# Second mixture of experts: row scatters spread over the next stage, weight sums in bfloat16 and one step later, the first expert's weight steps moved

## The chip, the cores and the metric

One core of one Trainium2 chip. The metric is the device time of one execution in microseconds (us). TensorE (PE) does the matrix products, VectorE (DVE), ScalarE (ACT) and GpSimd (POOL) the elementwise work; SyncE (SP) issues most transfers, POOL the indirect ones. Each engine takes its instructions in the order in which they are written and waits on semaphores.

## The reference, cut to what matters

The program does three things in a row: attention in chunks of 64, a mixture of experts in which each token goes to one expert, and a second mixture in which every token goes through every expert, with weights from 8 normalisations of rows and columns. The change touches only the second:

```
def _moe2_ref(x, w_gate, w1, w2):      # x: 2304 x 512, w1: 8 x 512 x 1024, w2: 8 x 1024 x 512
    logits = x @ w_gate
    P = np.exp(logits - logits.max())
    for _ in range(8):
        P /= P.sum(1, keepdims=True) + 1e-09
        P /= P.sum(0, keepdims=True) + 1e-09
        P *= N / E
    out = np.zeros((N, D))
    for e in range(E):
        out += P[:, e:e + 1] * (np.maximum(x @ w1[e], 0.0) @ w2[e])
```

The products are made from 16-bit halves: an operand is scaled by a power of two and split into a high and a low float16 part, and three of the four products of parts are added up. The power of two comes from the sum of the squares of the whole weight matrix.

## The kernel before, in words

**Loops.** The second mixture runs over 8 experts, `x = 0..7` in the code; an expert has 3 stages, `s = 0..2`, of 768 tokens. A stage has a first half (`x @ w1`, seven block products for each of four column groups `q`, 28 of six matmuls each, L1104) and a second half (times `w2`). The first expert (`plain`) does its second half as six plain products, `t = 0..5` (`second`, L1233, 24 matmuls of 512 columns each); the other seven do it by Strassen's scheme (`strassen`, L1189): seven products of 36 matmuls, in the order m = 1, 5, 6, 3, 7, 2, 4.

**Steps.** What else must be done is hung on numbered steps of a stage: `plan(s, i, f)` puts f behind step i of stage s, and `tick` runs it there. Steps 0 to 27 are the block products of the first half, step 28 + n follows the n-th product of the second half. Nothing runs by itself at a step: the number only sets where the instructions stand in the order of their engines.

**Elementwise work of the first half.** For a column group, ACT copies products out of PSUM to a tile `tq` (L1144 to L1146), DVE adds others to them (L1119), ACT makes the high parts `eh` (L1109), and the low parts `el` are made by DVE (`low`, L1112) or, from the second expert on, four of seven by POOL (`rest`, L1116). There are two `tq` tiles, taken in turn by the column groups; a group's copy waits until the last reader of the group two before it is done.

**The next expert's weights.** While expert x runs, matrices "b" (`w2`) and "a" (`w1`) of expert x + 1 are loaded to one staging buffer (L155, SP queue), squared and summed by ACT in four quarters (`w_stat`, L166, one column of `mx` each), summed over the partitions by a float32 matmul against ones (`w_scale`, `over_partitions`, L175: lhsT `ones32`, four columns, into the PSUM bank `p_l`), turned to a power of two by DVE (`w_scale2`, L189 and L89 to L92), and split in four pieces (`w_quad`): POOL makes the block sums into a `tq` tile (L252), ACT the high parts (L273), DVE the low parts (L274). Two of the four pieces of "b" are parked in DRAM (`b_away`, L1253) and fetched back at the next expert (`b_back`). For the first expert of this mixture the "b" matrix is split plainly during its first stage (`w_split`).

**The first expert** also turns the tokens by transposing transfers, makes the seven token blocks (`x_first` in its first stage by PE, step numbers in `build`; `x_sums` after), and computes the row and column normalisations (`sink_...`, DVE with an L175 sum on PE, the `scs` ones).

**The end.** Each stage's rows of the sum `acc` get the last expert's share by `into` (L1171). In the last expert `scatter` (L1176) follows at once: an indirect transfer from POOL for each of the stage's six row blocks, three behind product m = 2 and three behind m = 4.

## Time and profile before

| what | value |
|---|---|
| three runs | 1826.03, 1829.67, 1833.31 us (median 1829.67) |
| the profiled execution | 1826.54 us, span 1824.8 us |
| mean granted TensorE clock | 0.975 of full speed |
| busy in the span | PE 94%, PE weight loads 68%, DVE 66%, ACT 52%, POOL 39% |
| chain that ended last | PE 65%, DVE 4%, ACT 4% |

The span is the profiled execution from its first to its last instruction; the 1.7 us around it are the start and the end. Where PE is at work nearly all the time, what counts is where it stands still, and why. Times in the rows are from the span's start; the second mixture begins at about 414 us.

### The profile page before, as it was taken

Reading aid. Unit: us, or ns where it says so; the run is one execution under the profiler, and the core shown is the slowest. Engines: PE = TensorE matmul, PEld = TensorE weight load, DVE = VectorE, ACT = ScalarE, POOL = GpSimd, SP = SyncE. Lnnn points to the kernel's source line nnn. Section 1 sums busy time; section 2 is a strip of 40 time slices with the busy share of each in tenths; the row PEclk is TensorE's granted clock in tenths of the full one; section 3 lists DMA queues with packets and bytes.
Section 4 is the critical chain, followed back from the end, with each engine's and each line's share of the span. In section 5 each row is a group of like instructions: output and inputs, shape, how many; then the busy total and the mean of one; then the engine's idle time right before and its main releaser. Section 6 shows DMA issues by size and latency. Waiting matters only on the chain.

```text
span 1824.8 us, 33023 instructions
## 1 busy us (share of the span) xinstructions
PE 1715.4 (94%) x13025; PEld 1236.3 (68%) x13025; DVE 1199.6 (66%) x2341; ACT 957.5 (52%) x1806; POOL 709.9 (39%) x750
## 2 busy tenths in 40 slices
PE   7878999888899899999999999999999999999985
PEld 6766666655355477777777777777777777777654
DVE  5996657755456576676677667667766776675652
ACT  7964656754334465564465445555644655452330
POOL 1344335540011144353455345453433543443432
PEclk9978999999999899999999999999999999999997
DMA  9846566834324222332314224323313142222200
GB/s 237 209 158 219 164 191 162 226 118 131 127 44 155 83 91 80 121 124 92 128 62 168 87 82 161 108 82 108 138 71 128 62 170 99 92 97 79 79 35 35
DMA packets 140905, 219.17 MB, mean 120 GB/s; under 512 B 62881, under 2 KB 81393, under 8 KB 140721
## 3 DMA queue, kind: packets, MB, share of 16 engines
q1 hardware_dynamic: 133728, 198.92, 33.9%
q0 software_dynamic: 5360, 17.24, 2.9%
q8 instruction: 115, 1.88, 0.4%
q10 hardware_dynamic: 1632, 0.56, 0.1%
q14 instruction: 70, 0.57, 0.1%
HBM read 167.56 MB, written 41.91 MB: 115 GB/s over the span
## 4 chain that ended last, share of the span: by engine, by line
PE 65%; DVE 4%; ACT 4%; issue 2%; DMA 1%; POOL 0%; POOLq 0%; DVEq 0%; ACTq 0%
PE p_m L1104 34%; PE p_m L1189 26%; PE p_m L1233 4%; ACT wsq L166 3%; DVE tq L1122 2%; DVE acc L1171 1%; DMA out_dram<-acc,rk 1%; ACT eh L1109 1%; DVE wall L274 0%; PE p_m L992 0%; POOL el L1116 0%; PE p_l L175 0%; DVE tq L1119 0%; DVE el L1112 0%; ACT wall L231 0%
## 5 line engine op out<-in xcount | busy, mean ns | idle before, releaser
L1104 PE MATMUL p_m<-x,wall 128*128 128x384 f16 x4032 | 673.0, 328 | 18.2 <-ACT tq L1144 13.7
L1104 PEld LDWEIGHTS <-wall 128*128 128x128 f16 x4032 | 396.2, 98 | 279.7 <-issue 25.7
L1189 PE MATMUL p_m<-wall,eh 128*128 128x256 f16 x3528 | 580.6, 273 | 0.0
L1116 POOL TENSOR_TENSOR el<-tq,eh 128x384 f16<-128x384 f32 x336 | 344.6, 1053 | 558.8 <-ACT eh L1109 558.4
L1189 PE MATMUL p_m<-wall,el 128*128 128x256 f16 x1764 | 480.8, 273 | 0.0
L1109 ACT ACTIVATE eh<-tq 128x384 f16<-128x384 f32 x540 | 273.9, 522 | 200.9 <-DVE tq L1122 101.4
L1189 PEld LDWEIGHTS <-eh 128*128 128x128 f16 x3528 | 345.3, 98 | 44.3
L1171 DVE SCALAR_TENSOR_TENSOR acc<-p_m,cf,acc 128x256 f32<-128x256 f32 (+1 forms) x378 | 175.8, 521 | 181.1 <-PE p_m L1189 181.1
L1119 DVE TENSOR_TENSOR tq<-p_m,tq 128x384 f32<-128x384 f32 x288 | 159.1, 556 | 149.5 <-PE p_m L1104 143.6
L1189 PEld LDWEIGHTS <-el 128*128 128x128 f16 x1764 | 172.6, 98 | 19.9
L1112 DVE SCALAR_TENSOR_TENSOR el<-tq,eh 128x384 f16<-128x384 f32 x204 | 171.6, 844 | 8.3 <-ACT eh L1109 6.9
L1122 DVE SCALAR_TENSOR_TENSOR tq<-tq 128x384 f32<-128x384 f32 x252 | 133.0, 553 | 2.9
L1144 ACT COPY tq<-p_m 128x384 f32<-128x384 f32 x96 | 45.6, 475 | 153.6 <-PE p_m L1104 141.5
L742 PEld LDWEIGHTS <-wall 128*128 128x128 f16 x1152 | 106.0, 99 | 22.2 <-issue 7.0
L742 PE MATMUL p_p<-xT,wall 128*128 128x256 f16 x768 | 88.9, 277 | 6.3 <-DMA xT<-xg 2.1
L252 POOL TENSOR_TENSOR tq<-stb 128x256 f32<-128x256 f32 x56 | 47.6, 849 | 119.2 <-DVE el L1112 119.2
L1233 PE MATMUL p_m<-wall,eh 128*128 128x512 f16 x288 | 88.2, 389 | 0.0
L252 POOL TENSOR_TENSOR tq<-sta 128x256 f32<-128x256 f32 x56 | 41.2, 736 | 116.0 <-DVE el L1112 54.7
L1157 ACT ACTIVATE tq<-tq 128x384 f32<-128x384 f32 x84 | 43.9, 523 | 69.0 <-DVE tq L1119 69.0
L166 ACT ACTIVATE wsq<-sta 128x1024 bf16<-128x1024 f32 x64 | 67.5, 1054 | 1.5
L273 ACT ACTIVATE wall<-stb,wsb 128x256 f16<-128x256 f32 (+1 forms) x56 | 31.3, 606 | 68.1 <-DMA wb_d<-wall 41.8
L274 DVE SCALAR_TENSOR_TENSOR wall<-stb,wsb,wall 128x256 f16<-128x256 f32 (+1 forms) x56 | 41.3, 749 | 33.5 <-ACT wall L273 32.0
(258 smaller groups left out, 2107.9 us busy)
## 6 DMA issues: line engine op xcount, KB each, us to landing
x<-xt_d SPq DMA_DIRECT2D x147, 384.0 KB, 3.6
sta<-in_moe_w_dram SPq DMA_DIRECT2D x18, 1024.0 KB, 6.8
stb<-in_moe_w_dram SPq DMA_DIRECT2D x18, 1024.0 KB, 8.8
wb_d<-wall SPq DMA_DIRECT2D x20, 896.0 KB, 3.6
wall<-wb_d SPq DMA_DIRECT2D x20, 896.0 KB, 6.3
sta<-in_moe_w_dram SPq DMA_DIRECT2D x28, 512.0 KB, 7.6
stb<-in_moe_w_dram SPq DMA_DIRECT2D x28, 512.0 KB, 11.7
xt_d<-x SPq DMA_DIRECT2D x21, 384.0 KB, 3.8
```

Of the source, the lines that this page charges most:

```text
L166: nc.scalar.activation(out=sq, in_=src, func=AF.Square, accum_out=m.mx[:, h:h + 1])
L252: nc.gpsimd.tensor_tensor(out=at(o), in0=at(u), in1=at(v), op=op)
L742: nc.tensor.matmul(p[:, f4, :], lhsT=w[:, kk, f * 128:(f + 1) * 128], rhs=xT[:, lo + kk, 0:W], start=(n == 0), stop=(n == 3 * KD - 1))
L1104: nc.tensor.matmul(p, lhsT=wt[:, w, lw, kk, :], rhs=xt[:, lx, kk, :], start=first and n == 0, stop=n == 5, skip_group_check=not first)
L1109: nc.scalar.activation(out=hs[op][0][:, q, :], in_=src, func=AF.Relu if op in (A11, A12, A22) or plain else AF.Copy)
L1112: nc.vector.scalar_tensor_tensor(out=hs[op][1][:, q, :], in0=src, scalar=0.0, in1=hs[op][0][:, q, :], op0=ALU.max, op1=ALU.subtract)
L1116: nc.gpsimd.tensor_tensor(out=hs[op][1][:, q, :], in0=src, in1=hs[op][0][:, q, :], op=ALU.subtract)
L1119: nc.vector.tensor_tensor(out=o, in0=a, in1=b, op=ALU.add)
L1122: nc.vector.scalar_tensor_tensor(out=o, in0=a, scalar=0.0, in1=b, op0=ALU.max, op1=op)
L1171: nc.vector.scalar_tensor_tensor(out=acc[:, j, cols], in0=y, scalar=coefs[x][:, j:j + 1], in1=acc[:, j, cols], op0=ALU.mult, op1=ALU.add)
L1189: nc.tensor.matmul(bk.t[:, cols], lhsT=hs[op][lh][:, q, t * 128:(t + 1) * 128], rhs=b.q[q][:, w, lw, :], start=m in (1, 5) and q == 0 and ...
L1233: nc.tensor.matmul(y.t, lhsT=h[:, kk % 4, c * 128:(c + 1) * 128], rhs=w[:, kk, :], start=(n == 0), stop=(n == 3 * KF - 1))
```

## The change

Four things, all in the second mixture. (1) In the last expert, the scatters of stages 0 and 1 are written behind steps 3, 6, 10, 13, 17 and 20 of the next stage; the six of the last stage stay. (2) `w_sum`: DVE adds the four columns of `mx` to one bfloat16 number per partition, and the matmul is one of one column against a bfloat16 matrix of ones; `w_scale` and `w_scale2` now stand together at step 31, one product later than `w_scale` did. (3) Under the first expert, the next expert's "b" is summed and split during stage 1 (before: end of stage 0), and its "a" is loaded at the end of stage 1 and summed during the first half of stage 2 (before: loaded at its start, summed at its end); the pieces are made at steps 28 to 31. (4) In its first stage, two of four quarters of `w_split` go to POOL, and token block T4 is made at step 8 instead of 6.

```
@@ -101,6 +101,8 @@
     nc.vector.tensor_scalar(out=nid16, in0=ident, scalar1=-1.0, scalar2=None, op0=ALU.mult)
     ones32 = const.tile([128, 128], F32, name="ones32")
     nc.vector.memset(ones32, 1.0)
+    onesb = const.tile([128, 128], BF16, name="onesb")
+    nc.vector.memset(onesb, 1.0)
     cap_i = const.tile([128, 2], I32, name="cap_i")
     cap = const.tile([128, 1], F32, name="cap")
 
@@ -175,10 +177,21 @@
         nc.tensor.matmul(o, lhsT=ones32, rhs=src)
         return o
 
+    def w_sum(x, nm):
+        m = mats[x, nm]
+        m.all = small.tile([128, 1], BF16, tag="wall" + nm, name="wsumsq")
+        with nc.allow_low_precision(reason="chooses a power of two"):
+            nc.vector.tensor_reduce(out=m.all, in_=m.mx, axis=AX.X, op=ALU.add)
+
     def w_scale(x, nm):
         m = mats[x, nm]
         m.scaled = False
-        m.am = over_partitions(m.mx, {"a": 288, "b": 292}[nm], 4)
+        at = {"a": 288, "b": 292}[nm]
+        if hasattr(m, "all"):
+            m.am = sums["bank"][:, at:at + 1]
+            nc.tensor.matmul(m.am, lhsT=onesb, rhs=m.all)
+        else:
+            m.am = over_partitions(m.mx, at, 4)
 
     def w_scale2(x, nm):
         m = mats[x, nm]
@@ -186,7 +199,10 @@
         m.s, m.inv = smw("ws" + nm, [128, 1]), smw("wi" + nm, [128, 1])
         if x not in iws:
             iws[x] = smw("iw", [128, 1])
-        nc.vector.tensor_reduce(out=mm, in_=m.am, axis=AX.X, op=ALU.add)
+        if hasattr(m, "all"):
+            mm = m.am
+        else:
+            nc.vector.tensor_reduce(out=mm, in_=m.am, axis=AX.X, op=ALU.add)
         if m.ssq:
             pow2_of_sumsq(mm, LF, small.tile([128, 1], I32, tag="wh", name="wh"), m.s, m.inv)
         else:
@@ -1171,8 +1187,11 @@
         nc.vector.scalar_tensor_tensor(out=acc[:, j, cols], in0=y, scalar=coefs[x][:, j:j + 1], in1=acc[:, j, cols],
                                        op0=ALU.mult, op1=ALU.add)
 
-    def scatter(j):
-        if x == E - 1:
+    def scatter(j, later=True):
+        if x == E - 1 and later and j < NT - 6:
+            s, t = divmod(j, 6)
+            plan(s + 1, 3 + 7 * (t // 2) + 3 * (t % 2), lambda: scatter(j, False))
+        elif x == E - 1:
             nc.gpsimd.indirect_dma_start(out=out[:, :], out_offset=bass.IndirectOffsetOnAxis(ap=rk[:, j, 1:2].bitcast(I32), axis=0),
                                          in_=acc[:, j, :], in_offset=None)
 
@@ -1242,6 +1261,7 @@
         m = mats[x, "b"]
         if q == 0:
             bounced.clear()
+            m.at = {}
         i = spare[q % len(spare)]
         m.q[q] = quad_slot(i).rearrange("p (c l n) -> p c l n", c=7, l=2)
         m.at[q] = i
@@ -1255,7 +1275,7 @@
 
     def b_back(x):
         m = mats[x, "b"]
-        taken = [m.at[q] for q in range(4 - len(bounced) * 0) if q >= len(bounced)]
+        taken = [m.at[q] for q in range(len(bounced), 4)]
         rest_of = [i for i in range(5) if i not in taken]
         for q, r0 in bounced:
             i = rest_of.pop(0)
@@ -1270,7 +1290,7 @@
                 f()
 
     x_rows(0, (B12,))
-    build = {0: (B11, T1), 1: (T2,), 3: (B22,), 4: (B21,), 5: (T3,), 6: (T4,)}
+    build = {0: (B11, T1), 1: (T2,), 3: (B22,), 4: (B21,), 5: (T3,), 8: (T4,)}
     for x in range(E):
         cur, nxt = E + x, E + x + 1
         plain = x == 0
@@ -1284,23 +1304,26 @@
                 f()
 
         if x + 1 < E:
-            for h in range(2):
-                plan(0, h + (14 if x == 0 else 1), lambda h=h: w_load(nxt, "b", h))
-                plan(2, h, lambda h=h: w_load(nxt, "a", h))
-            for h in range(4):
-                plan(0, 29 + h // 2, lambda h=h: w_stat(nxt, "b", h, True))
-                plan(2, 29 + h // 2, lambda h=h: w_stat(nxt, "a", h, True))
-            for s, nm in ((0, "b"), (2, "a")):
-                plan(s, 30, lambda nm=nm: w_scale(nxt, nm), lambda nm=nm: w_alloc(nxt, nm))
-                plan(s, 31, lambda nm=nm: w_scale2(nxt, nm))
-            mats_at = lambda: setattr(mats[nxt, "b"], "at", {})
-            plan(0, 30, mats_at)
-            for q in range(4):
-                s, i = (0, 1)[q // 2], (31, 32, 29, 31)[q]
-                plan(s, i, lambda q=q: w_quad(nxt, "b", q, 0), lambda q=q: b_slot(nxt, q), lambda q=q: w_quad(nxt, "b", q, 1),
-                     lambda q=q: w_quad(nxt, "b", q, 2), lambda q=q: b_away(nxt, q))
-                plan(2, (31, 32, 33, 33)[q], lambda q=q: w_quad(nxt, "a", q, 0), lambda q=q: w_quad(nxt, "a", q, 1),
-                     lambda q=q: w_quad(nxt, "a", q, 2))
+            def matrix(nm, load, stat, scale, quads):
+                for h in range(2):
+                    plan(*load[h], lambda h=h: w_load(nxt, nm, h))
+                for h in range(4):
+                    plan(*stat[h], lambda h=h: w_stat(nxt, nm, h, True))
+                (s0, i0), (s1, i1) = scale
+                plan(s0, i0, lambda: w_sum(nxt, nm))
+                plan(s1, i1, lambda: w_scale(nxt, nm), lambda: w_scale2(nxt, nm), lambda: w_alloc(nxt, nm))
+                for q in range(4):
+                    plan(*quads[q], lambda q=q: w_quad(nxt, nm, q, 0), lambda q=q: nm == "b" and b_slot(nxt, q),
+                         lambda q=q: w_quad(nxt, nm, q, 1), lambda q=q: w_quad(nxt, nm, q, 2),
+                         lambda q=q: nm == "b" and b_away(nxt, q))
+
+            at = lambda s, *ii: [(s, i) for i in ii]
+            if x == 0:
+                matrix("b", at(0, 14, 15), at(1, 3, 8, 13, 18), at(1, 22, 24), at(1, 28, 29, 30, 31))
+                matrix("a", at(1, 33, 33), at(2, 5, 10, 15, 20), at(2, 22, 24), at(2, 28, 28, 29, 30))
+            else:
+                matrix("b", at(0, 1, 2), at(0, 29, 29, 30, 30), at(0, 30, 31), at(0, 31, 32) + at(1, 29, 31))
+                matrix("a", at(2, 0, 1), at(2, 29, 29, 30, 30), at(2, 30, 31), at(2, 31, 32, 33, 33))
         if x > 0:
             plan(0, 0, lambda: b_back(cur))
         if x == 1:
@@ -1324,8 +1347,8 @@
         if x == 0:
             plan(0, 1, lambda: w_scale(E, "b"))
             plan(0, 2, lambda: w_scale2(E, "b"))
-            for h in range(4):
-                plan(0, 2 * h + 5, lambda h=h: w_split(E, "b", h, 4))
+            for i, h in ((5, 1), (6, 0), (8, 3), (10, 2)):
+                plan(0, i, lambda h=h: w_split(E, "b", h, 4, 2 * (h % 2)))
         for s in range(NSB):
             hs = h_tiles((A11, A12, A22, S1) if plain else range(7))
             slots = {}
```

**POOL in the last expert**, its stages 0 to 1 (the `el` rows are the low parts of a column group, four to a group, told apart by their `tq`; `out_0_dram` is the output). Before:

```order
L1116 TENSOR_TENSOR el_22331<-tq_22537,eh_22330 128x384
L1176 DMA out_0_dram<-acc_8920,rk_8921 2304x512 x6
L1116 TENSOR_TENSOR el_22924<-tq_22938,eh_22923 128x384
L1116 TENSOR_TENSOR el_22928<-tq_22938,eh_22927 128x384
L1116 TENSOR_TENSOR el_22926<-tq_22938,eh_22925 128x384
L1116 TENSOR_TENSOR el_22930<-tq_22938,eh_22929 128x384
L1116 TENSOR_TENSOR el_22924<-tq_22989,eh_22923 128x384
```

and now:

```order
L1132 TENSOR_TENSOR el_22349<-tq_22555,eh_22348 128x384
L1195 DMA out_0_dram<-acc_8922,rk_8923 2304x512 x2
L1132 TENSOR_TENSOR el_22936<-tq_22950,eh_22935 128x384
L1132 TENSOR_TENSOR el_22940<-tq_22950,eh_22939 128x384
L1132 TENSOR_TENSOR el_22938<-tq_22950,eh_22937 128x384
L1132 TENSOR_TENSOR el_22942<-tq_22950,eh_22941 128x384
L1195 DMA out_0_dram<-acc_8922,rk_8923 2304x512 x2
L1132 TENSOR_TENSOR el_22936<-tq_23003,eh_22935 128x384
L1132 TENSOR_TENSOR el_22940<-tq_23003,eh_22939 128x384
L1132 TENSOR_TENSOR el_22938<-tq_23003,eh_22937 128x384
L1132 TENSOR_TENSOR el_22942<-tq_23003,eh_22941 128x384
```

Six scatters in a row stood ahead of the next stage's low parts; two stand there now, and two behind each of the first two groups.

**ACT under the first expert**, from the last casts of `x_sums` in stage 0 on (`wsq` is the sum of squares, `wall` a piece of the next weights, `acc` the result of a plain product, `tq` and `eh` belong to the first half of stage 1). Before:

```order
L958 CAST x_9541<-xsum 128x768
L166 ACTIVATE wsq,wmxb<-stb_9274 128x1024 x2
L1235 COPY acc<-p_m 128x512
L166 ACTIVATE wsq,wmxb<-stb_9274 128x1024 x2
L1235 COPY acc<-p_m 128x512
L273 ACTIVATE wall<-stb_9274,wsb 128x256
L273 ACTIVATE wall<-stb_9274,wsb 128x2x256
L273 ACTIVATE wall<-tq,wsb 128x4x256
L1235 COPY acc<-p_m 128x512
L273 ACTIVATE wall<-stb_9274,wsb 128x256
```

and now:

```order
L974 CAST x_9545<-xsum 128x768
L1254 COPY acc<-p_m 128x512 x4
L1160 COPY tq<-p_m 128x384
L1161 COPY tq<-p_m 128x384
L1162 COPY tq<-p_m 128x384
L168 ACTIVATE wsq,wmxb<-stb_9278 128x1024
L1125 ACTIVATE eh<-tq 128x384 x3
L1160 COPY tq<-p_m 128x384
L1161 COPY tq<-p_m 128x384
L168 ACTIVATE wsq,wmxb<-stb_9278 128x1024
```

The sums of squares and the pieces that stood among the plain products of stage 0 are gone from there; the sums stand one to a column group in stage 1, and the pieces follow 32 rows further down, behind its plain products.

**DVE, matrix "b", first stage of the second expert** (`p_l` holds the sum over the partitions, `wsumsq` is the bfloat16 number). Before:

```order
L1171 SCALAR_TENSOR_TENSOR acc<-p_m,cf_10968,acc 128x256 x6
L189 TENSOR_REDUCE wmmb<-p_l 128x1
L89 TENSOR_SCALAR wh<-wmmb 128x1
L90 TENSOR_SCALAR wsb<-wh 128x1
L92 TENSOR_SCALAR wib<-wh 128x1
L274 SCALAR_TENSOR_TENSOR wall<-stb_10901,wsb,wall 128x256
L274 SCALAR_TENSOR_TENSOR wall<-stb_10901,wsb,wall 128x2x256
L274 SCALAR_TENSOR_TENSOR wall<-tq,wsb,wall 128x4x256
```

and now:

```order
L1187 SCALAR_TENSOR_TENSOR acc<-p_m,cf_10974,acc 128x256 x6
L184 TENSOR_REDUCE wsumsq<-wmxb 128x1
L89 TENSOR_SCALAR wh<-p_l 128x1
L90 TENSOR_SCALAR wsb<-wh 128x1
L92 TENSOR_SCALAR wib<-wh 128x1
L290 SCALAR_TENSOR_TENSOR wall<-stb_10907,wsb,wall 128x256
L290 SCALAR_TENSOR_TENSOR wall<-stb_10907,wsb,wall 128x2x256
L290 SCALAR_TENSOR_TENSOR wall<-tq,wsb,wall 128x4x256
```

DVE's own sum moves ahead of the matmul, so that the exponent is taken from PSUM; the row count is the same, and the rows behind it are in the same order.

## Rows read from the trace of the kernel before

**Rows 1.** Chain that ended last, steady stages: start us, length us, engine and line.
```profile
687.88 26.32 PE p_m L1104 x162
714.21 3.93 PE p_m L1189 x36
...
742.69 26.33 PE p_m L1104 x162
...
798.10 26.32 PE p_m L1104 x162
```

**Rows 2.** Timeline of PE at a weight sum: start us, us, line, count, [idle before].
```profile
781.51 0.27 PE L1189 MATMUL p_m<-wall,el 128*128 128x256 f16 x1
781.98 0.39 PE L175 MATMUL p_l<-wmxa,ones 128*128 128x4 f32 x2 [0.19 <-ACT wsq L166]
782.22 0.38 PE L1189 MATMUL p_m<-wall,eh 128*128 128x256 f16 x2
```

**Rows 3.** Timelines of DVE, then ACT, behind that weight sum.
```profile
789.62 1.27 DVE L1171 SCALAR_TENSOR_TENSOR acc<-p_m,cf,acc 128x256 f32<-128x256 f32 x3 [3.08 <-PE p_m L1189]
...
793.55 2.07 DVE L1171 SCALAR_TENSOR_TENSOR acc<-p_m,cf,acc 128x512 f32<-128x512 f32 x3 [0.41 <-PE p_m L1189]
...
796.99 1.27 DVE L274 SCALAR_TENSOR_TENSOR wall<-tq,wsa,wall 128x1024 f16<-128x1024 f32 x1
...
799.11 0.48 ACT L1144 COPY tq<-p_m 128x384 f32<-128x384 f32 x1 [1.81 <-PE p_m L1104]
```

**Rows 4.** Chain that ended last: starts of the last expert's stages 1 and 2.
```profile
1681.03 5.86 PE p_m L1104 x36
...
1741.73 12.69 PE p_m L1104 x78
```

**Rows 5.** Timeline of POOL in the last expert, stages 0 and 1.
```profile
1641.05 4.14 POOL L1116 TENSOR_TENSOR el<-tq,eh 128x384 f16<-128x384 f32 x4 [2.54 <-ACT eh L1109]
...
1684.77 0.96 POOL L1176 DMA_INDIRECT out_dram<-acc,rk  x1 [2.71 <-DMA out_dram<-acc,rk]
...
1696.68 3.50 POOL L1116 TENSOR_TENSOR el<-tq,eh 128x384 f16<-128x384 f32 x4
```

**Rows 6.** Timeline of PE in the last expert, stages 1 and 2: its two idle times.
```profile
1700.75 4.54 PE L1104 MATMUL p_m<-x,wall 128*128 128x384 f16 x17 [4.12 <-ACT tq L1144]
...
1762.39 3.04 PE L1104 MATMUL p_m<-x,wall 128*128 128x384 f16 x9 [5.06 <-ACT tq L1144]
```

**Rows 7.** Chain that ended last: starts of the first expert's stages 1 and 2.
```profile
500.68 26.32 PE p_m L1104 x162
...
560.25 3.91 PE p_m L1104 x24
```

**Rows 8.** Timeline of PE under the first expert: its idle times, and where the second expert starts.
```profile
432.96 2.12 PE L1104 MATMUL p_m<-x,wall 128*128 128x384 f16 x12 [1.38 <-DVE tq L1119]
...
443.28 7.69 PE L1104 MATMUL p_m<-x,wall 128*128 128x384 f16 x36 [2.36 <-DVE tq L1119]
...
481.67 0.59 PE L175 MATMUL p_l<-wmxb,ones 128*128 128x4 f32 x2 [7.73 <-ACT wsq L166]
...
606.97 0.39 PE L175 MATMUL p_l<-wmxa,ones 128*128 128x4 f32 x2 [2.78 <-ACT wsq L166]
...
624.72 2.11 PE L1104 MATMUL p_m<-x,wall 128*128 128x384 f16 x12
631.38 6.17 PE L1104 MATMUL p_m<-x,wall 128*128 128x384 f16 x24 [4.55 <-ACT tq L1144]
```

**Rows 9.** Windows: us, busy us (x) of PE, PEld, DVE, ACT, POOL, granted clock, DMA, GB/s.
```profile
630.00:634.00 4.00, 2.62 (x9) 1.23 (x9) 3.02 (x4) 1.81 (x4) 0.00 (x0) 0.50 0.30 78
```

**Rows 10.** DMA issues, 550 to 562 us: count, KB each, median us to landing.
```profile
sta<-in_moe_w_dram SPq DMA_DIRECT2D x2, 1024.0 KB, 8.3
```

**Rows 11.** Lines L224 and L274: count, duration ns min/median/max, first and last start.
```profile
L224 POOL TENSOR_SCALAR stb<-stb,wsb x14: 2839/2847/3812, 155.3 to 362.5; 128x1024 f32<-128x1024 f32 x14
...
L274 DVE SCALAR_TENSOR_TENSOR wall<-sta,wsa,wall x64: 470/743/1295, 384.7 to 1627.0; 128x512 f16<-128x512 f32 x32, 128x256 f16<-128x256 f32 x32
```

## The prediction

> **What bounds the kernel now.** I read the page first: PE is busy 94% of the span, so the second mixture can only lose time where PE stands still or runs at the lower clock. The waits of PE from 400 us on then name three causes, and the chain and the timelines show the places. A steady stage, one without a weight sum, is PE from end to end: it starts at 687.88 and the next at 742.69, 54.81 us, and nothing is to be had there [rows 1]. A stage with a weight sum takes 742.69 to 798.10, 55.41 us: 0.60 more [rows 1], and the timeline shows where it goes. The last matmul ahead of the sum starts at 781.51, the next product's first one at 782.22, 0.71 later [rows 2], where 36 matmuls of this form otherwise take 3.93, 0.11 each [rows 1]. PE waited there for the last ACT square and then made two float32 passes (x2).
>
> The dear places are elsewhere. Under the first expert PE waits 7.73 us for the squares of "b", 2.78 us for those of "a", and 4.55 us at the second expert's first group, where ACT is behind with the pieces of "a" [rows 8]. In the last expert it waits 4.12 and 5.06 us for an ACT copy [rows 6] that waits for a `tq` tile; the tile is held by POOL, whose low parts start at 1696.68 only because six scatters stand ahead of them, each held until the one before has landed (2.71 us, and 0.96 to issue) [rows 5]. After such waits PE runs for a while at 1.2 instead of 2.4 GHz: the granted clock is 0.50 in the window from 630 us [rows 9].
>
> **The change part by part**, against the profiled execution (1826.54 us, 3.1 below the median of the runs).
>
> *Scatters.* What they cost now is the length of a last-expert stage over a steady one: 1681.03 to 1741.73 is 60.70 [rows 4], less 54.81 is 5.9. Of that 4.12 is waiting [rows 6], so 1.8 is the low clock behind it; stage 2 has 5.06 of waiting [rows 6], with the same 1.8 it makes 6.9. Sum 12.8 us. What the moved scatters cost: POOL has 2.54 us free ahead of the second group's low parts [rows 5]. Two scatters there take 0.96 + 2.71 + 0.96 = 4.6 us, as the second waits for the first to land, so these low parts start 2.1 us late and the third group's, by the same sum, 4.2; the fourth group has nothing ahead of it. Is that late for anyone? The stage of the rows starts at 1681.03 - 54.81 = 1626.2, a block product takes 6 x 26.32/162 = 0.975 us [rows 1], and the second group's low parts end at 1645.2 [rows 5], 19.0 into the stage. The next to want its tile is the copy behind product 21, 20.5 into the stage, and PE wants the bank that this copy frees two products later: 1.5 + 2.0 us of cover for 2.1. The third group's tile is wanted in the next stage, its low parts behind a whole product of the second half. The two scatters behind steps 3 and 6 meet an idle POOL. I take 0.4 us back: gain 12.4.
>
> *Weight sums, second to seventh expert.* Twelve places at 0.60 us. A bfloat16 sum of one column is not in the trace: its cost lies between 0 and that of the two float32 passes, 782.22 - 781.98 = 0.24 [rows 2]; one pass of two, 0.12, is the nearest. The wait goes, since the matmul stands one product later, 3.93 us [rows 1], and DVE's sum, in place of the one that it made afterwards, needs only the squares. 12 x 0.48 = 5.8 us. What the later place costs: the scale comes some 3.4 us later (3.93 less the wait and the passes), and with it all pieces on ACT and DVE. DVE stood idle 3.08 us ahead of the next `into` and 0.41 ahead of the one after [rows 3]; these cover it, so that the third piece of "a" still ends near 798.3 (now 796.99 + 1.27) and the copy that takes its tile starts at 799.11 [rows 3], by then some 0.5 us earlier. That leaves next to nothing in the six "a" places: I take 0.5 us back in all.
>
> *"b" under the first expert.* The squares stood behind the casts of `x_sums` on ACT, among the plain products. They now stand one to a column group of stage 1, where ACT has room: a stage is 59.57 us there (500.68 to 560.25 [rows 7]). The 7.73 us go [rows 8], and the low clock with them, which I price by the same event of "a": stage 2 takes 560.25 to 624.72 [rows 7, 8], 64.47, against 59.57 for stage 1; of these 4.9, 2.78 is the wait, so 2.1 the rest. 9.8 us. Late next: the parked pieces. The second parked piece now leaves behind seven stores on SP's queue, and the fourth piece must wait for it on ACT; queued behind it on ACT are only copies of plain products, which have PSUM banks to spare.
>
> *"a" under the first expert.* The 4.9 us go. Late next: its load is issued when the last "b" piece has been read, about when stage 2 starts; it lands 8.3 us later [rows 10], and the first square stands behind six block products, 5.9 us into the stage. ACT may wait about 2.4 us, with copies behind it that have two products, 2.0 us, until PE wants the bank. And the four pieces now stand among the normalisation steps, whose sums PE asks for once in a plain product, every 5.4 us (59.57 less 28 x 0.975, in six). I take 1 us back for both.
>
> *Second expert's start.* It takes 624.72 to 687.88 [rows 1, 8], 63.16 us, against 54.81 + 0.60: 7.75 us over. The pieces of "a" are now made three plain products, some 16 us, earlier, so ACT is free: 7.7 us go.
>
> *First stage's split.* PE waits 1.38 and 2.36 us for DVE adds [rows 8]; 36 matmuls behind the second take 7.69 instead of 36 x 26.32/162 = 5.85 us, 1.8 of low clock. DVE loses two of four pieces and the second wait has no piece ahead of it any more. But T4, made two steps later, is wanted in the very next step, behind a DVE piece: a new wait, for which the nearest row is the 2.36 us of such a backlog now. Bounds: a gain of 5.5 (1.38 + 2.36 + 1.8, all of it) to a loss of 3 (a third wait of this size); I take 2, the second wait gone and the third there in part.
>
> POOL gets two quarters at 2.85 us for the scaling [rows 11] and about as much for the difference, some 10 us in a stretch in which it did nothing. While POOL works, DVE's pieces of 256 to 512 columns take between 470 and 1295 ns [rows 11], so its work could stretch DVE's. GPSIMD Engine Reference, Key points, in the Trainium skill, says why: GpSimd shares its SBUF interfaces with VectorE and contends with instructions that have two SBUF inputs. By that rule the move gives back what it takes off DVE; the spread of those durations speaks for it, so it is a rival below.
>
> Sum: 12.4 + 5.8 - 0.5 + 9.8 + 4.9 - 1.0 + 7.7 + 2.0 = 41.1 us; 1826.5 - 41.1 = 1785.4. A median run stands 3.1 above the profiled one, so the time lies at 1785 to 1789: I forecast **1787**, a chance of 0.64.
>
> **The rivals.**
> - *The first expert gives half back* (0.15): "a" lands late, or PE's normalisation sums wait for DVE, which now has four pieces between them. For it: a piece takes DVE 1.27 [rows 3] and two of 0.74 us [rows 11], 2.8, and two pieces and a normalisation stand at one step of 5.4. Against it: the steps after it hold one piece each or none. A new wait of 3 to 4 us with its 2 us of low clock, twice: 10 us back, 1797.
> - *The scatters still hold the low parts* (0.09): if a landing takes 5 us rather than 2.7, the second group is 4.4 us late, over its 3.5 of cover, and PE waits 1 us with 1.8 of low clock behind it, in both stages: 6 us back, 1793.
> - *POOL's quarters slow DVE* (0.06): the waits of 1.38 and 2.36 us stay and a third joins them, so that the 2 us of gain become the 3 of loss: 1792.
> - *Slower* (0.04): the sum that stands a product later pushes the pieces over the stage's end. Place: the copy at 799.11 and the PSUM bank behind it, twelve times. It decides once the 3.4 us meet less than some 1.5 us of idle DVE; the 3.49 in the rows speak against it. Price: 3 us of waiting and 1.8 of low clock, 12 x 4.8 = 58 instead of a gain of 5.3; the other parts' 35.8 stay: 1826.5 + 58 - 35.8 = 1849.
> - *It does not do what it says* (0.02): the waits are inferred, and another semaphore releases PE at the same time. Then 1826. Against it: each idle time ends with the end of the named ACT work.
>
> **How the numbers follow.** The forecast's own range, from its unknown costs (split 5.5 to -3, the 0 to 0.24 us of a sum, the 1.9 us taken back left out or doubled), is 1781 to 1794. With the first three rivals it is **1780 to 1800**, which leaves out the last two and the tails. About 0.5%, 9 us, is what a measurement of this kernel can tell from none: every case but the last two is beyond it, so faster 0.94, the same 0.02, slower 0.04.
>
> **What would show it.** Right: no PE wait for `wsq` at all; second halves of first-expert stages of equal length; steady stages all near 54.9 us; the second expert's first stage near 55; the last expert's three stages alike, with scatters in pairs between the low parts, and one POOL wait for a landing in each pair. Wrong: a PE wait for an ACT copy at the start of a stage behind "a" pieces (the slower rival), a wait of ACT for the load of "a" early in stage 2 followed by one of PE, PE waits at `scs` sums, or PE idle at T4 in the first stage longer than 3.7 us.

## The result, and the profile after

The changed kernel takes 1801.68 us (median of four runs, 1794.23 to 1808.11), the kernel before 1828.48 on the same chip: a ratio of 0.985, interval 0.980 to 0.989. A second session gave 1801.03 against 1833.54, 0.983 (0.980 to 0.986). It is faster, as forecast, but by 26.8 and 32.5 us (1.5 and 1.7%) and not by 41, and its median lies 1.7 us above the range of 1780 to 1800.

The page of the changed kernel's profiled execution (1794.23 us) has PE busy for 95% of a shorter span; POOL got a little more to do:

```profile
span 1792.5 us, 32997 instructions
...
PE 1697.2 (95%) x13011; PEld 1228.1 (69%) x13011; DVE 1201.9 (67%) x2340; ACT 955.9 (53%) x1806; POOL 729.2 (41%) x754
```

PE's waits from 405 us to the end (who waits, for what: us in all, times, longest) are what is left of [rows 2, 6, 8]. The waits for `wsq` are gone, all fourteen, and so are the long ones for copies of line 1160 (1144 before) but one; the first row, at the second mixture's first product, was there before. New are those for `wsumsq`, for `scs`, for `x` (the token block T4) and for `el`, and six short ones among the seven for line 1160:

```profile
PE p_m L1008 <- SPq L892: 5.1, 1, 5.1
PE p_m L1120 <- ACT tq L1160: 4.9, 7, 2.5
PE p_m L1120 <- DVE tq L1135: 1.6, 1, 1.6
PE p_l L192 <- DVE wsumsq L184: 1.2, 1, 1.2
PE p_l L177 <- DVE scs L1089: 1.0, 1, 1.0
PE p_m L1120 <- ACT x L1029: 0.9, 1, 0.9
PE p_m L1120 <- ACT tq L1162: 0.5, 1, 0.5
PE p_m L1208 <- DVE el L1128: 0.5, 1, 0.5
PE p_m L1120 <- DVE x L1030: 0.3, 1, 0.3
```

The chain, in short stretches, gives the starts of stages (start us, length in the stretch): the first expert's stage 1, the second expert's two first stages, the last expert's stages 1 and 2. They answer to [rows 4, 7, 8]:

```profile
490.12 9.91 PE p_m L1120 x61
...
670.49 1.62 PE p_m L1120 x10
...
1660.68 3.41 PE p_m L1120 x21
...
1716.15 1.95 PE p_m L1120 x12
```

I read the length of every stage in every run the same way, from the first matmul of its first block product to that of the next stage's (PE's timeline; a start lies some 0.2 us ahead of the chain's). Stages that nothing disturbs repeat to 0.02 us, so that these lengths tell apart what whole times, which scatter by 10 us, cannot. Of e6, e7, e9, e10 and e11 there is one run each, the profiled one, and they are read by stage lengths alone. The table has all runs, the experiments' too: "x" is the start of the second mixture (first matmul of line 992, now 1008), then in us stages 0, 1, 2 of the first expert, stage 0 of the second, stages 0 and 2 of the fourth (which stand for the third to seventh), stages 1 and 2 of the last, and the time from x to the end of the span.

| run | x | 1st: 0 | 1 | 2 | 2nd: 0 | 4th: 0 | 2 | last: 1 | 2 | x to end |
|---|---|---|---|---|---|---|---|---|---|---|
| before | 413.85 | 86.66 | 59.58 | 64.63 | 63.00 | 55.41 | 55.40 | 60.71 | 61.43 | 1410.95 |
| after | 416.51 | 73.44 | 59.61 | 65.15 | 55.62 | 55.40 | 54.83 | 55.46 | 54.70 | 1375.99 |
| e1 after again | 420.35 | 74.06 | 59.61 | 65.17 | 55.61 | 55.38 | 54.84 | 56.11 | 54.70 | 1377.25 |
| e2 park | 429.65 | 73.91 | 59.60 | 62.52 | 55.61 | 55.38 | 54.83 | 55.37 | 54.70 | 1373.75 |
| e3 park, norm | 424.27 | 74.21 | 59.61 | 59.79 | 55.61 | 55.38 | 54.83 | 56.34 | 54.70 | 1372.33 |
| e4 own tile | 422.83 | 73.82 | 59.61 | 65.17 | 55.61 | 54.83 | 54.84 | 55.35 | 54.70 | 1372.97 |
| e5 before again | 425.74 | 86.01 | 59.59 | 62.93 | 62.58 | 55.40 | 55.41 | 60.57 | 61.14 | 1407.76 |
| e6 old split | 425.33 | 75.22 | 59.61 | 66.64 | 55.61 | 55.39 | 54.84 | 56.35 | 54.70 | 1380.17 |
| e7 early a | 418.26 | 73.68 | 59.60 | 65.19 | 55.61 | 54.84 | 55.76 | 55.21 | 54.70 | 1378.24 |
| e8 all together | 420.42 | 74.31 | 59.61 | 59.79 | 55.61 | 54.83 | 54.84 | 54.81 | 54.70 | 1367.88 |
| e9 sum step | 429.17 | 73.91 | 59.60 | 61.11 | 55.62 | 55.39 | 54.83 | 55.32 | 54.70 | 1372.33 |
| e10 T4 early | 419.30 | 73.98 | 59.61 | 65.16 | 55.62 | 55.39 | 54.83 | 56.08 | 54.70 | 1377.10 |
| e11 float32 late | 423.07 | 74.24 | 59.60 | 65.19 | 55.73 | 55.66 | 54.95 | 55.31 | 54.70 | 1378.93 |

Three places fall short. **Stage 2 of the first expert** is no shorter. Timelines of ACT and PE (start us, us, [idle before, until]) show ACT held 6.04 us by the parked piece's store, and PE behind it, then twice behind DVE:

```profile
550.63 1.12 ACT L289 ACTIVATE wall<-stb,wsb 128x256 f16<-128x256 f32 x2 [6.04 <-DMA wb_d<-wall]
...
554.18 2.11 PE L1120 MATMUL p_m<-x,wall 128*128 128x384 f16 x12 [2.51 <-ACT tq L1160]
...
577.72 0.16 PE L192 MATMUL p_l<-wsumsq,onesb 128*128 128x1 bf16 x1 [1.23 <-DVE wsumsq L184]
...
598.66 0.39 PE L177 MATMUL p_l<-scs,ones 128*128 128x8 f32 x2 [1.04 <-DVE scs L1089]
```

SP's queue and DVE's timeline show why the store is late. The second one is issued at 543.28, behind the seven stores of x and 15.3 us after the first. But these stores did not keep it back: DVE, busy with `x_sums` until 540.5, had finished this piece only at 542.90. What is slow is the store itself. It lands 7.27 us after its issue (the chain's row), where the first, with none of these stores ahead of it, took 3.8; ACT gets on 7.35 us after the issue. These 3.5 us more are enough for all of PE's wait; that the stores of x still under way made them fits, but was not tested apart:

```profile
527.98 0.52 SPq L1273 DMA_DIRECT2D wb_d<-wall  x1
528.55 14.64 SPq L946 DMA_DIRECT2D xt_d<-x  x7
543.28 1.08 SPq L1273 DMA_DIRECT2D wb_d<-wall  x1
...
541.62 1.28 DVE L290 SCALAR_TENSOR_TENSOR wall<-tq,wsb,wall 128x1024 f16<-128x1024 f32 x1
...
543.28 7.27 DMA wb_d<-wall
```

**The "a" places** of the steady experts gain nothing: the third stages, where their sums stand, fell to 54.83, but the first stages, where the "b" sums stand and should have fallen too, stayed at 55.40: the "a" pieces now hold up their start. DVE's, ACT's and PE's timelines at such a place: DVE ends the low parts of the third piece's sums (the 1024 columns, from a `tq` tile) at 781.86, the next stage's first copy waits for that tile, and PE for the copy. In [rows 3] the copy waited for PE.

```profile
780.59 1.27 DVE L290 SCALAR_TENSOR_TENSOR wall<-tq,wsa,wall 128x1024 f16<-128x1024 f32 x1
...
781.96 0.48 ACT L1160 COPY tq<-p_m 128x384 f32<-128x384 f32 x1 [0.38 <-DVE wall L290]
...
782.49 17.71 PE L1120 MATMUL p_m<-x,wall 128*128 128x384 f16 x108 [0.40 <-ACT tq L1160]
```

The third piece ends 56.73 us into its stage, which starts at 725.13; before it was 55.73 (796.99 + 1.27, less 742.53). DVE's idle time took up the later scale; this one microsecond comes on top. DVE's six rows of the first three pieces take 9.21 us now and took 8.11 before, and the rows that grew run beside POOL's block sums. Here is the second piece's row now, the POOL row beside it, and the same DVE row before, when POOL stood still:

```profile
775.21 1.74 DVE L290 SCALAR_TENSOR_TENSOR wall<-tq,wsa,wall 128x1024 f16<-128x1024 f32 x1
...
774.97 0.90 POOL L268 TENSOR_TENSOR tq<-sta,tq 128x256 f32<-128x256 f32 x1
...
791.86 1.28 DVE L274 SCALAR_TENSOR_TENSOR wall<-tq,wsa,wall 128x1024 f16<-128x1024 f32 x1
```

**The last expert's stage 1** is 55.46, not 54.81. POOL's timeline has the scatters in pairs between the low parts, as meant, but the second of the third pair is held 3.57 us by the landing of the one before; where [rows 5] had six scatters in a row ahead of low parts, here it is this pair. The low parts that come late then run beside a low part of DVE's, which takes 3.08 us instead of 0.55, and PE waits for that one (POOL's, DVE's and PE's timelines):

```profile
1680.99 1.11 POOL L1195 DMA_INDIRECT out_dram<-acc,rk  x1 [0.16 <-issue]
1685.66 0.97 POOL L1195 DMA_INDIRECT out_dram<-acc,rk  x1 [3.57 <-DMA out_dram<-acc,rk]
1686.65 3.52 POOL L1132 TENSOR_TENSOR el<-tq,eh 128x384 f16<-128x384 f32 x4
...
1687.52 3.08 DVE L1128 SCALAR_TENSOR_TENSOR el<-tq,eh 128x384 f16<-128x384 f32 x1
...
1690.65 0.28 PE L1208 MATMUL p_m<-wall,el 128*128 128x256 f16 x1 [0.48 <-DVE el L1128]
```

### The profile page after: what moved, and what is told of

Read it like the earlier page. It is cut to its first block, busy times and chain, and to the rows that moved or that the text cites. A ratio compares the mean times of both kernels' runs of the same rounds, so it can differ in the third digit from the quotient of the medians.

```text
span 1792.5 us, 32997 instructions
## 1 busy us (share of the span) xinstructions
PE 1697.2 (95%) x13011; PEld 1228.1 (69%) x13011; DVE 1201.9 (67%) x2340; ACT 955.9 (53%) x1806; POOL 729.2 (41%) x754
## 4 chain that ended last, share of the span: by engine, by line
PE 66%; DVE 6%; ACT 2%; DMA 1%; issue 1%; SPq 1%; POOLq 0%; DVEq 0%; ACTq 0%
PE p_m L1120 34%; PE p_m L1208 28%; DVE wall L290 3%; PE p_m L1252 3%; DVE acc L1187 1%; ACT wall L289 1%; DMA out_dram<-acc,rk 1%; DVE xsum L969 1%; SPq L955 1%; DVE el L1128 0%; DMA wb_d<-wall 0%; PE p_m L1008 0%; DVE tq L1135 0%; ACT eh L1125 0%; DMA x<-x_d 0%
## 5 line engine op out<-in xcount | busy, mean ns | idle before, releaser
L1120 PEld LDWEIGHTS <-wall 128*128 128x128 f16 x4032 | 393.9, 98 | 266.9 <-issue 12.4
L268 POOL TENSOR_TENSOR tq<-sta 128x256 f32<-128x256 f32 x56 | 45.1, 805 | 76.7 <-DVE wall L290 44.2
```

The source lines that it names most:

```text
L268: nc.gpsimd.tensor_tensor(out=at(o), in0=at(u), in1=at(v), op=op)
L1120: nc.tensor.matmul(p, lhsT=wt[:, w, lw, kk, :], rhs=xt[:, lx, kk, :], start=first and n == 0, stop=n == 5, skip_group_check=not first)
```

## The experiments

**e1: the changed kernel again**, without an edit.

> The changed kernel once more, to see which parts of its shortfall repeat. Theory (the shortfall is in three kinds of place: ACT held by the second parked piece of "b", late normalisation sums in the first expert's stage 2, and the six "a" places that gain nothing): the stages from the first expert's stage 1 on have the lengths of the first profile within 0.5 us (the two stages of the first expert 124.8, a steady expert 165.0, the last expert's two stages 55.5 and 54.8), the parked piece again lands 7 us after its issue, and what differs between the two profiles lies ahead of the second mixture. Rival (the changed kernel varies in itself): the parked piece's landing or the load of "a" differs by over 2 us, and the second mixture's length, 1376.0 us in the first profile from the first matmul of the first product to the end, moves by over 3 us. Time by either: 1794 to 1808, median near 1800.

Median 1801.03 us (1798.87 to 1805.72). The stages repeat: 124.78 for the first expert's last two, 165.03 for the fourth expert, the same waits of 2.5, 1.2 and 1.1 us there. Only the last expert's stage 1 moved, 55.46 to 56.11, and the first expert's stage 0 by 0.6. The second mixture is 1.26 us longer, its start 3.84 later. The rival falls: what varies most lies ahead of the changed code.

**e2: the second parked piece one step earlier.**

```diff
-matrix("b", at(0, 14, 15), at(1, 3, 8, 13, 18), at(1, 22, 24), at(1, 28, 29, 30, 31))
+matrix("b", at(0, 14, 15), at(1, 3, 8, 13, 18), at(1, 22, 24), at(1, 28, 28, 30, 31))
```

> The changed kernel with the second parked piece of the first expert's "b" made one step earlier, beside the first, so that both stores are issued ahead of the seven stores of x, and nothing else. Theory: ACT no longer waits 6.04 us for that store, the copies of stage 2's first group run when PE has written them, PE's wait of 2.51 us at the start of stage 2 and the low clock behind it (some 1.5 us) go: 3 to 4 us less than the changed kernel, stage 1 and 2 of the first expert together 121 instead of 124.8. Rival (the wait for the store hides another that ends as late, the piece's turn behind DVE or POOL): the PE wait stays over 1.5 us under another name and the time is that of the changed kernel within 1 us.

Stage 2 fell from 65.17 to 62.52, and its start has no wait; the copy waits for PE now, as it should (PE's and ACT's timelines):

```profile
563.16 6.01 PE L1120 MATMUL p_m<-x,wall 128*128 128x384 f16 x36
...
564.34 0.48 ACT L1160 COPY tq<-p_m 128x384 f32<-128x384 f32 x1 [0.39 <-PE p_m L1120]
```

So the late store was the cause, worth 2.65 us, little more than the wait of 2.51. The edit moves the piece and its store together, so it does not divide the lateness between the piece, made behind `x_sums`, and the slow landing. I had expected 3 to 4: the low clock that I added was not there. The whole time (median 1802.52) is that of the changed kernel; the profiled run starts the second mixture late (429.65), and the starts of the other four are not known. From x to the end it takes 1373.75 us, 2.9 less than the mean of after's two.

**e3: in addition "a" scaled at step 26, one piece to a step.**

```diff
-matrix("a", at(1, 33, 33), at(2, 5, 10, 15, 20), at(2, 22, 24), at(2, 28, 28, 29, 30))
+matrix("a", at(1, 33, 33), at(2, 5, 10, 15, 20), at(2, 22, 26), at(2, 28, 29, 30, 31))
```

> As the kernel with the second parked piece moved, and the scale of the first expert's "a" four block products later (step 26 instead of 24) with its pieces one to a step (28, 29, 30, 31) instead of two at the first of these steps. Theory (two normalisation sums of PE come late because DVE has a weight sum or two pieces ahead of the sum's source): the waits of 1.2 and 1.0 us in stage 2 go, 2 to 3 us less than the kernel with the piece moved alone, since each also cost a while of low clock. Rival (pieces one step later are late for the second expert's start): PE waits there for an ACT copy, over the 0.5 us that it waited, and what is won in stage 2 is lost again, the time that of the kernel with the piece moved within 1 us.

Both waits are gone. Stage 2 takes 59.79 us, 2.73 less, within 0.2 of stage 1, and the second expert's stage 0 did not move (55.61). Median 1796.85.

**e9: only the scale's step of e3** (pieces left at 28, 28, 29, 30).

> The kernel with the second parked piece moved, and of the second edit under the first expert only its first half: the scale of "a" at step 26 instead of 24, its pieces left at steps 28, 28, 29, 30. This divides the 2.7 us by which stage 2 of the first expert became shorter (62.52 to 59.79) between the late weight sum (a wait of 1.2 us) and the two pieces ahead of a normalisation (a wait of 1.1). Theory (each wait has its own cause): the wait for wsumsq goes and that for scs stays, stage 2 lasts 61.0 to 61.4. Rival (the pieces are late because the scale is, and the wait for scs is its result or grows with a later scale): the wait for scs goes as well, or it grows to over 2 us and stage 2 lasts as long as without the edit, over 62.2.

61.11 us: the two waits are independent, 1.41 and 1.32 us. PE's timeline has no wait at the weight sum, and still one at the normalisation:

```profile
588.74 0.17 PE L192 MATMUL p_l<-wsumsq,onesb 128*128 128x1 bf16 x1
...
607.74 0.39 PE L177 MATMUL p_l<-scs,ones 128*128 128x8 f32 x2 [1.05 <-DVE scs L1089]
```

**e4: a tile of its own for the sums of the fourth "a" piece.**

```diff
-wsum = m.sums[q] = wsums[q % len(wsums)] if wsums else sums_of[0]()
+wsum = m.sums[q] = wsums[q % len(wsums)] if wsums else own[0] if own and nm == "a" and q == 3 else sums_of[0]()
...
+own.append(ep.tile([128, 4, 2, 128], F32, name="own"))
...
-dg = ep.tile([128, 128], F32, name="sdg")
+dg = wall[:, 9 * QW:9 * QW + 256].bitcast(F32)
```

> The changed kernel with a third tile for the sums that POOL makes for the fourth piece of every "a" in the second mixture, so that these sums and the next stage's first copies no longer share two tiles (the diagonal matrix of the row maximum moves to an unused part of the weights' tile to make room). Theory (the six "a" places gain nothing because the next stage's first ACT copy waits for the tile that DVE frees with the third piece): the copy no longer waits, the 0.40 us of PE and what stands behind it go in six places, steady experts 164.5 instead of 165.04, in all 2 to 4 us less than the changed kernel. Rival (ACT and DVE are behind by themselves, with the pieces, whatever tile they use): the copy is then held by the pieces ahead of it on ACT, PE's wait stays within 0.2 us, no gain over 1 us.

First stages from the third expert on take 54.83 us, 0.55 less each, as long as an undisturbed stage; PE's waits for line 1160's copies (1162 there) are gone. So PE was held there through the tile alone; with a third tile ACT and DVE are in time with the later pieces. From x to the end 1372.97, 3.65 less than the mean of after's two.

**e7: the sum of "a" one product earlier again, still in bfloat16.**

```diff
-matrix("a", at(2, 0, 1), at(2, 29, 29, 30, 30), at(2, 30, 31), at(2, 31, 32, 33, 33))
+matrix("a", at(2, 0, 1), at(2, 29, 29, 30, 30), at(2, 30, 30), at(2, 31, 32, 33, 33))
```

> The changed kernel with the sum of every "a" from the second expert on at step 30, one product earlier, where it stood before the change; it stays a bfloat16 sum of one column. Theory (the later place costs in the "a" places what it wins, since the pieces end later): the copy at the next stage's start is no longer held, first stages of the third to seventh expert take 54.83 us instead of 55.39, and the third stages take 55.2 to 55.4 instead of 54.83, because PE again waits 0.4 to 0.5 us for the squares: the time is that of the changed kernel within 1 us, the bfloat16 sum alone is worth 0.0 to 0.2 us a place. Rival (something else holds the copy, not the later pieces): first stages stay at 55.39 and third stages rise, 2 to 4 us slower.

The first half held: first stages 54.84, so the copy is held only by later pieces. But the third stages take 55.77, not 55.2 to 55.4, more than before the change (55.41): PE waits longer, since ahead of the matmul stands not only the last square but DVE's sum of it. PE's timeline, to be held against the 0.19 us and the two float32 matmuls of [rows 2]:

```profile
767.17 0.16 PE L192 MATMUL p_l<-wsumsq,onesb 128*128 128x1 bf16 x1 [0.77 <-DVE wsumsq L184]
```

At this earlier place DVE's six rows of the first three pieces take 8.11 us again, as before the change.

**e11: float32 sums at the later place** (no `w_sum` but for the second expert's weights).

> The changed kernel with the weight sums of the second to the eighth expert in float32 again, two passes of four columns and DVE's sum behind them, at the later place. With the bfloat16 sum at the early place (third stages 55.76, first 54.84) it separates the number format from the place. Theory (the place is what pays where it pays; the format is worth the passes alone): third stages last 54.9 to 55.0 instead of 54.83, first stages 55.4 to 55.6, together 0.1 to 0.3 us a place, 1 to 3 us over the second mixture. Rival (without DVE's sum ahead of the matmul the scale comes as early or earlier, so that the format gives nothing): third stages within 0.05 of 54.83 and first stages at or below 55.39.

Third stages 54.95, first stages 55.66: the theory's size, the second a little above its range. The two float32 matmuls cost 0.12 us of PE in each stage. At the "a" place the pieces come later by another 0.15 (55.66 - 55.39 - 0.12); that this is DVE's sum behind the matmuls, 0.16 us long, fits but was not tested apart. There is no wait at the sum (PE's timeline):

```profile
775.66 0.28 PE L177 MATMUL p_l<-wmxa,ones 128*128 128x4 f32 x2
```

**e6: the old split, and e10: only T4 at its old step.** e6 puts the quarters at steps 5, 7, 9, 11 on DVE and T4 at 6; e10 is

```diff
-build = {0: (B11, T1), 1: (T2,), 3: (B22,), 4: (B21,), 5: (T3,), 8: (T4,)}
+build = {0: (B11, T1), 1: (T2,), 3: (B22,), 4: (B21,), 5: (T3,), 6: (T4,)}
```

> The changed kernel with the split of the first "b" undone: its quarters at steps 5, 7, 9, 11 in their order, all on DVE, and T4 made at step 6. Theory (the quarters that went to POOL took DVE's backlog away): the first half of the first expert's first stage, from its first product of x to its first second product, takes 43.4 us as before instead of 40.3 to 41.0, with PE waits of 1.4 and 2.4 us for DVE adds. Rival (the gain there came from T4 or from the squares that no longer stand in this stage): it stays under 41.5 us.

> The changed kernel with T4 made at step 6 again and the quarters of the first "b" left as changed, two of them on POOL. It divides what the split's part is worth (1.3 us in the first half of the first stage, 38.25 with the old split against 36.9 to 37.15). Theory (POOL's two quarters do it, T4's place is worth little): 36.8 to 37.4 us. Rival (T4's place does it, as its adds met DVE's pieces at step 6): 38 us or more, with a PE wait of over 2 us for a DVE add.

From x on e6 takes 41.97 us, between theory and rival; 3.72 of it are the first products of x, which vary by 0.7 from run to run. Without these, from the first block product on, it is 38.25 us with the old split, 36.92 after the change (36.91 in e1) and 37.28 with T4 early, where a wait for a DVE add of 2.7 us stands in place of shorter ones. So the split's part is worth 1.3 us, three quarters of it by POOL's quarters. In e5 the same stretch of the kernel before takes 38.24, so the squares that left the stage play no part in its first half. In the first profile of the kernel before it takes 39.79 with the same two waits: there PE ran at the lower clock behind the second one (7.69 us for 36 matmuls [rows 8], 6.01 in e5), and against that profile the split's part is 2.9. The waits for DVE adds behind it are those of [rows 8], here in PE's waits from 425 to 470 us of e6:

```profile
PE p_m L1120 <- DVE tq L1135: 3.7, 2, 2.4
```

**e5: the kernel before again.**

> The kernel before once more, for a second profile of it. In the five profiles of the changed kernel and its variants the second mixture's first product started at 416.5, 420.4, 429.7, 424.3 and 422.8 us, in code that the change does not touch; in the one profile of the kernel before at 413.85. Theory (the start varies from execution to execution, whatever the kernel, and the first profile of the kernel before was an early one): the second mixture from its first product to the end lasts 1411.0 us within 1, every stage as in the first profile within 0.1, and the start lies later than 413.85, near 420, since the times of this kernel have a median of 1833.5 here. Rival (the change itself delays the first part, by a constant more and other places in the memory): the start is again 414 within 2.

The start lies at 425.74, 11.9 us later than in the profile on which the prediction was made, in the same kernel: the theory's main point. The view of line 992 (duration ns min/median/max, first and last start) has the same durations as there, all later:

```profile
L992 PE MATMUL p_m<-id,wall x96: 216/219/314, 425.7 to 440.4; 128*128 128x128 f16 x96
```

Against the theory, the second mixture took 1407.76 us and not 1411 within 1: stages with long waits of PE are up to 1.7 us shorter (62.93 instead of 64.63), the others the same.

**e8: the parts together, and the last expert's scatters in two groups.** The edits of e3 and e4, and

```diff
-plan(s + 1, 3 + 7 * (t // 2) + 3 * (t % 2), lambda: scatter(j, False))
+plan(s + 1, (1, 4, 28, 29, 30, 31)[t], lambda: scatter(j, False))
```

> All found so far in one kernel: the second parked piece one step earlier, the first expert's "a" scale at step 26 and its pieces one to a step, the third tile for the sums of the fourth "a" piece, and of the six scatters of each of the last expert's first two stages two in the next stage's first group (steps 1 and 4) and four in its second half (steps 28 to 31), where POOL has nothing to do. Theory: the parts add up, 1.9 + 2.7 + 3.4 us in the second mixture as measured apart, and the last expert's second stage comes from 55.4 to 56.3 down to 54.9: the second mixture lasts 1367 to 1369 us, 8 to 9 less than the changed kernel's 1376.0 and 1377.25, and the time is near 1792. Rival (the parts take from one another: moved pieces meet the second expert's start, scatters in the second half meet the last six): the second expert's first stage grows over 56 us, or the end behind PE's last matmul grows over 22.5 us, and under 5 us are won.

Median 1789.96 us (1788.07 to 1791.56), a ratio of 0.977 to the kernel before (0.9745 to 0.9793), below both intervals of the changed kernel; from x to the end 1367.88, as forecast. No wait for line 1160's copies (1162 here), `wsumsq`, `scs` or `el` is left; the last expert's stage 1 takes 54.81. POOL's timeline there: low parts back at 2.69 us of waiting for ACT, scatters from 1693 on with nothing behind them.

```profile
1678.77 4.13 POOL L1134 TENSOR_TENSOR el<-tq,eh 128x384 f16<-128x384 f32 x4 [2.69 <-ACT eh L1127]
1689.10 4.14 POOL L1134 TENSOR_TENSOR el<-tq,eh 128x384 f16<-128x384 f32 x4 [6.20 <-ACT eh L1127]
1693.39 0.97 POOL L1197 DMA_INDIRECT out_dram<-acc,rk  x1 [0.15 <-issue]
1696.37 0.97 POOL L1197 DMA_INDIRECT out_dram<-acc,rk  x1 [2.00 <-DMA out_dram<-acc,rk]
```

## Why the prediction was wrong, point by point

Measured is what the table gives, before less after, for the two pairs (first profiles; e5 and e1). The prediction's 0.48 us for the "b" sum inside the second expert's first stage is put with that stage here.

| step | forecast | first pair | second pair |
|---|---|---|---|
| scatters: last expert's stages 1, 2 | 12.4 | 12.0 | 10.9 |
| weight sums, the other eleven places | 4.8 | 3.0 | 3.0 |
| "b" under the first expert and the split: stage 0 | 11.8 | 13.2 | 12.0 |
| "a" under the first expert: stages 1, 2 | 3.9 | -0.6 | -2.3 |
| second expert's first stage | 8.2 | 7.4 | 7.0 |
| sum | 41.1 | 35.0 | 30.5 |

The direction and most mechanisms were right. The waits for `wsq` fell everywhere. The last expert's stage 1 is 0.4 to 1.5 us over an undisturbed one in the runs with scatters in pairs, where the prediction took back 0.4 for both stages: it priced late low parts of POOL's by who reads their tile, and not by the DVE instruction that runs beside them. The split's 2 us were 1.3, or 2.9 against the first profile, and that they come near is in part luck: T4's new wait was 1.2 us (0.86 and 0.31, for `x`), but the second wait did not go; it is 1.6 us and ends right behind a DVE instruction that POOL's work made 1.6 us longer (last section).

**The step that failed is the cost of what I moved under the first expert.** For "b" I saw that the second parked piece would leave behind seven stores and that the fourth piece would wait for it on ACT, and then wrote that the copies queued behind it "have PSUM banks to spare", and took nothing. The copies of plain products had; but behind them the same ACT queue holds the next stage's first copy, which has not, and PE stood 2.51 us (e2: 2.65 of stage 2). For "a" I took 1 us for a late load and for the normalisation sums together. The load was no cost (ACT's first square of "a", at 559.03, waits for nothing); the sums were 1.41 and 1.32 us (e9, e3), since in one case DVE has the weight sum queued behind `sink_rows`, and in the other two pieces ahead of it. Without these three, stage 2 takes 59.79, and the gain of stages 1 and 2 against the two profiles of before, 4.8 and 3.1 us, brackets the forecast of 3.9. Two of the signs that I had listed as wrong did show: PE waits at `scs` sums, and a PE wait for an ACT copy at the start of a stage behind "a" pieces. My rival "the first expert gives half back" had named the normalisation, and its 10 us were too many.

**The weight sums** were mis-sized: 0.48 a place with 0.5 us given back in all. The "b" places won 0.58, more than forecast, as the bfloat16 matmul took only 0.02 us of the stage; the six "a" places won 0.01. I had the third piece of "a" end "near 798.3" and the copy start some 0.5 us before 799.11, so by 0.3 us in time. DVE's idle time did cover the later scale; what I left out is that the pieces, in their new place, run beside POOL's block sums and take 1.1 us more on DVE (9.21 for 8.11, and 8.11 again in e7). The third piece ended 1.0 us later, and the copy was held 0.38. e4 shows the tile as the cause, and with it the whole 0.57 a place is there. The rival "slower" had this place and this mechanism, not its size.

**The level** was the third point of the shortfall. The prediction set its sum against a profile whose second mixture began at 413.85 us, and added 3.1 us at most for the median. The eleven profiles of the changed kernel and its variants begin it between 416.5 and 429.7, 422.65 on average, and e5 shows that the kernel before does the same. Of the 14.7 us between forecast and median about 8.4 are gain that did not come (41.1 less 32.7, the mean of the pairs), the other 6 or so go with this start, 8.8 us later on average, which three times had not shown. What makes the first part vary was not tried. The granted clock goes with it: from PE's first work on the gathered tokens (142.87, 147.47 and 148.11 us) to x the first profile of the kernel before takes 270.98 us at 0.97, e5 278.27 at 0.96 and e2 281.54 at 0.95. Its scatter of some 13 us had no place in the range. Nor do the bounds of the forecast's own range follow from the costs that it lists: added up they give 1780 to 1795, not 1781 to 1794, which changes nothing here.

## What to carry to other kernels

When a step moves to another place in the program, follow each of its instructions down its in-order queue to the first one that PE wants: a wait there that is harmless in itself costs PE as soon as one such copy stands behind it. Look also at what it now runs beside: the same DVE instructions grew by 1.1 us next to POOL's. Moving a sum behind its source pays only if the steps that follow have both time and a tile; a shared pair of tiles ate the whole gain in half of the places here. And where one part of a program varies from run to run, compare the lengths of the stages, which repeat to 0.02 us, and put the variable part's scatter into the range.

## What the runs showed of the hardware

**The same wait of PE may or may not cost clock.** The prediction added about 2 us of low clock to each long wait (1.8 in the last expert, 2.1 for "a"). Behind the 2.51 us wait at 554 us of the changed kernel the granted clock was 1.00, behind the same wait of 2.50 us in e6 it was 0.66, and stage 2 was 1.5 us longer (66.64 to 65.15). Windows (us, busy us (x) of PE, PEld, DVE, ACT, POOL, granted clock, DMA, GB/s) of the changed kernel, then of e6:

```profile
554.00:557.00 3.00, 2.82 (x18) 1.72 (x18) 2.24 (x8) 1.00 (x4) 0.00 (x0) 1.00 0.99 365
```

```profile
565.00:570.00 5.00, 5.00 (x22) 2.57 (x21) 2.83 (x8) 1.10 (x3) 0.00 (x0) 0.66 0.97 397
```

The kernel before does the same without any edit: around its wait of 2.78 us for the squares of "a" the granted clock was 0.80 in the first profile and 1.00 in e5, and there lies the 1.7 us between their stages 2 (64.63 and 62.93). So the clock's part of a gain read from one profile is a bound, not a figure:

```profile
606.00:610.00 4.00, 3.03 (x12) 1.38 (x13) 0.75 (x3) 0.92 (x2) 0.00 (x0) 0.80 0.00 0
```

```profile
617.20:621.20 4.00, 2.98 (x15) 1.50 (x16) 0.80 (x3) 0.97 (x2) 0.00 (x0) 1.00 0.00 0
```

**A POOL instruction can hold up one of DVE until it is done.** In the first stage of the changed kernel two DVE instructions that otherwise take 0.55 us took 2.37 and 2.15, each ending within 0.45 us of the POOL difference that it met. PE waited for the add behind the second one (DVE's, POOL's and PE's timelines):

```profile
435.71 2.37 DVE L1128 SCALAR_TENSOR_TENSOR el<-tq,eh 128x384 f16<-128x384 f32 x1
...
441.27 2.15 DVE L1128 SCALAR_TENSOR_TENSOR el<-tq,eh 128x384 f16<-128x384 f32 x1 [0.59 <-ACT eh L1125]
...
435.53 2.13 POOL L241 TENSOR_TENSOR wall<-stb,wall 128x1024 f16<-128x1024 f32 x1
...
440.87 2.13 POOL L241 TENSOR_TENSOR wall<-stb,wall 128x1024 f16<-128x1024 f32 x1
...
443.34 1.01 DVE L1135 TENSOR_TENSOR tq<-p_m,tq 128x384 f32<-128x384 f32 x2
...
444.40 6.01 PE L1120 MATMUL p_m<-x,wall 128*128 128x384 f16 x36 [1.59 <-DVE tq L1135]
```

The same happened in two more places of this kernel, shown above: the "a" pieces and the last expert's low part. Which instructions are open to it can be read from all those of one line (count, duration ns min/median/max): with both inputs in SBUF tiles they take up to 3078 ns, with one of them in PSUM (`p_m`) never more than 559, though most of these run beside POOL too.

```profile
L1128 DVE SCALAR_TENSOR_TENSOR el<-tq,eh x204: 546/558/3078, 429.9 to 1748.5; 128x384 f16<-128x384 f32 x102
L1128 DVE SCALAR_TENSOR_TENSOR el<-p_m,eh x96: 539/547/559, 438.0 to 1750.2; 128x384 f16<-128x384 f32 x96
```

This agrees with the rule that the prediction weighed, GPSIMD Engine Reference, Key points, in the Trainium skill: GpSimd contends with VectorE instructions that have two inputs in SBUF. The rival built on it had the mechanism right and the size too large: POOL's work keeps a wait of 1.6 us in being, and yet the split's part won 1.3 us, most of it by the quarters that DVE no longer makes (e10).

**A one-column bfloat16 sum is nearly free, but not its source.** In a row of matmuls it took 0.02 us of the stage (54.83 to 54.81), the two float32 matmuls 0.12 more (e11); where PE has to wait for its source, DVE's extra sum made the place dearer than the float32 one, 55.77 to 55.41 (e7).
